# A linear-attention, gated-MLP and mixer kernel: state products on quarter tiles behind a TensorE drain, and preparation work moved between VectorE, ScalarE and GpSimd

## The chip, the core and the metric

One NeuronCore of one Trainium2 chip. The metric is the device time of one execution in microseconds (us), the median of several runs. All times here are in us unless ns is written. The engines are TensorE (PE, with its weight loads as PEld), VectorE (DVE), ScalarE (ACT), GpSimd (POOL) and SyncE (SP), whose queue issues the DMAs.

## What is computed

Three modules in a chain. The first is a linear attention with a forget gate, for 4 batches of 8 heads, 768 tokens and 48 columns a head:

```python
f = 1.0 / (1.0 + np.exp(-f_logit))
for t in range(S):
    state = f[:, :, t, :, None] * state + np.einsum('bhd,bhe->bhde', k[:, :, t], v[:, :, t])
    y[:, :, t] = np.einsum('bhd,bhde->bhe', q[:, :, t], state)
```

The second is a gated MLP over tokens: `h = relu(x @ w_in)` is split into `u` and `v`, `v` is normalised over its 512 columns, mixed over the tokens as `w_spatial @ v_n + b_spatial`, multiplied by `u`, and multiplied by `w_out`. The third is a mixer: `u = x + (relu(x^T @ w_tok1) @ w_tok2)^T`, then `u + relu(u @ w_ch1) @ w_ch2`, with 384 model columns, 256 token columns and 1536 channel columns.

## The kernel before

**Precision.** A product of two f32 matrices is made of three fast matmuls: each operand is split into a high part (rounded to the fast type) and a low part (what the rounding left), and L196, L197 and L198 issue high by high, low by high and high by low. Some small products in the attention run in plain f32, each as two matmul records in the trace.

**Weights.** They arrive as 64-bit numbers. `rounded` turns a piece of 128 x 384 of them into f32: a DMA of 384 KB, two VectorE instructions (L74, L77), one on ScalarE (L81), one on GpSimd (L83). Then ScalarE writes the high part (L156) and the engine that `split_weight` is given writes the low part (L159). The staging buffers `wst` and `wsa` are rings of three. Some weights are rounded early and stored back to DRAM as f32 by `round_weight` (w_tok1, w_tok2 and w_ch1; the tasks are called `later`), and loaded again, at half the bytes, where they are split (kind "narrow").

**Attention.** The work is cut into 32 units of one batch, one half of the sequence (six chunks of 64 tokens) and one pair of heads (`unit(k)`). Per unit, VectorE scans the gates (L332, L346) and scales `kq` (L352); TensorE makes `products`, `turns` and `keys`; ScalarE copies the products out (`am`, L393), GpSimd masks them (L398). VectorE sums the states chunk by chunk (L412). GpSimd multiplies all of a unit's states by the gates at the chunk ends and lays them out as block-diagonal matrices of both heads in `now` (L420, with a second multiplicand `pown` written by L340). On TensorE `past` (L429) multiplies `now` by the queries, one 112 x 112 matmul a chunk, five chunks in the first half of a sequence and six in the second. `sums` (L440) adds the part within the chunk to the same PSUM tile `py`. ScalarE and VectorE split the result into high and low (L461, L465).

The small products use the array as four quarter tiles of 64 x 64: `block(old, now, new)` issues `past` of one unit first, then walks round robin over four lists with the products and turns of a later unit, the keys of the next, and the sums. A chain on one quarter tile thus runs beside those on the other three.

**Order.** `settle` is a planner: every piece of work is a task with an engine, a cost, a rank and the buffers that it takes; the planner plays the queues forward and emits the task of lowest rank among those that can start soonest. Attention, gated MLP and weight pieces are mixed by it. `s1_tasks` makes the first half of the gated MLP: relu on ScalarE (`r`, L710), its statistics on VectorE (L714, L716), the inverse root on GpSimd (L722), the normalised `vf` on VectorE (L726), then high part `vh` on ScalarE (L734) and low part `vl` on VectorE (L737). The mix follows: `g` (L807, L808), `gh` (L813), `gl` (L818). The last stage (c1, c2, ff) is emitted in the order of the code, with weight pieces woven in by `staged`.

Every engine runs its instructions in the order in which they were emitted.

Of the kernel before, what the change touches and what calls it, by code (L numbers as in the profile page):

```python
# [9 lines left out]
F32 = mybir.dt.float32  # L10
# [9 lines left out]
def tile_kernel(ctx, tc, fkqs, v, w_in, w_sp, b_sp, w_out, w_t1, w_t2, w_c1, w_c2, out):  # L20
# [179 lines left out]
    def body(general):  # L200
# [42 lines left out]
        now = attp.tile([P, NT, 2, 64], F32, name="now")  # L243
        zs = [attp.tile([P, NT, D], F32, name=f"zs{i}") for i in range(NP)]
        own = attp.tile([P, 1, 2], F32, name="own")
        pown = attp.tile([P, B * NP, 2 * NT, 2], F32, name="pown")
        for t in [first, last, now, own]:
            nc.gpsimd.memset(t, 0.0)
        for j in range(2):
            nc.gpsimd.memset(own[64 * j : 64 * j + 64, :, j], 1.0)  # L250
# [13 lines left out]
        def scanned(u, b, hf, p, fs, kq, vt):  # L264
# [9 lines left out]
            vs = at2.tile([P, W], F32, tag="am", name=f"vs{u}")  # L274
# [31 lines left out]
        def unit(k):  # L306
# [30 lines left out]
            def ends():  # L337
                end = d["pg"][:, 1, T - 1 :: T]
                nc.gpsimd.tensor_copy(pend[:, b * NP + p, n0 : n0 + NT], end)
                nc.gpsimd.tensor_tensor(  # L340
                    out=pown[:, b * NP + p, n0 : n0 + NT], in0=end.unsqueeze(2).to_broadcast([P, NT, 2]),
                    in1=own.to_broadcast([P, NT, 2]), op=ALU.mult,
                )
# [73 lines left out]
            def scaled(eng):  # L417
                n = NT - 1 + hf
                x = n0 - hf
                eng.tensor_tensor(  # L420
                    out=now[:112, 1 - hf :, :, :D], in0=d["z"][:112, :n].unsqueeze(2).to_broadcast([112, n, 2, D]),
                    in1=pown[:112, b * NP + p, x : x + n].unsqueeze(3).to_broadcast([112, n, 2, D]), op=ALU.mult,
                )

            def past():

                py = d["py"]
                for c in range(1 - hf, NT):
                    nc.tensor.matmul(  # L429
                        py[:112, c % 2, c // 2 * T : (c // 2 + 1) * T],  # L430
                        now[:112, c].rearrange("p j e -> p (j e)")[:, :112], d["qi"][:112, toks(c)],
                        start=c + hf < 3, stop=False, skip_group_check=True,
                    )

# [53 lines left out]
        def block(old, now, new):  # L488
# [3 lines left out]
            if old:  # L492
                old["d"]["py"] = ps_y.tile([P, 2, 512], F32, tag="py", name="py")
                old["past"]()
# [6 lines left out]

            if new:
# [3 lines left out]
            if now:  # L506
                now["d"]["pk"] = pa
                add(now["keys"])
            if old:
                add(old["sums"])  # L510
            run(*tiles[::2], *tiles[1::2])
# [61 lines left out]
        def att_tasks(k, at):  # L573
# [18 lines left out]
            else:  # L592
                task(f"G{k}", "ACT", 0.65, at - 3.2, f["gate"], [f"L{k}", back1("SC")])
                task(f"SC{k}", "DVE", 1.17, at - 3, f["ahead"], [f"G{k}", back1("BK")], [("pg", 1, [f"MU{k}", f"PE{k}"])])
                task(f"PE{k}", "POOL", 0.45, at - 2.8, f["ends"], [f"SC{k}"])
# [3 lines left out]
                for r in range(2):  # L599
# [6 lines left out]
                eng, ns = "POOL", 1.4  # L606
                task(
                    f"NW{k}", eng, ns, at + 3, partial(f["scaled"], nc.gpsimd), [f"ST{k}"],
                    [("now", 1, [f"SU{k}"])],
                )  # L610
# [51 lines left out]
        def piece_tasks(name, gen, rank, width, kind, ring=True, after=()):  # L662
# [4 lines left out]
            if kind == "narrow":  # L667
                task(f"{name}d", "SP", 0.45, rank, step, after, kb=192 * r, rings=[("wsa", 3, [f"{name}l"])])
                task(f"{name}h", "ACT", 0.45 * r, rank + 2, step, [f"{name}d"])
                task(f"{name}l", "POOL", 1.05 * r, rank + 2, step, [f"{name}h"])  # L670
# [3 lines left out]
            last_use = {"pe": f"{name}t", "pool": f"{name}l", "store": f"{name}s"}[kind]  # L674
# [10 lines left out]
            else:  # L685
                task(f"{name}l", "POOL", 1.05 * r, rank + 1, step, [f"{name}h"])
# [4 lines left out]
        def s1_tasks(b, hf, places):  # L691
# [6 lines left out]
            def norm(i):  # L698
# [19 lines left out]
                def root():  # L718
# [3 lines left out]
                    nc.gpsimd.tensor_tensor(out=e["rs"], in0=ve, in1=nhalf, op=ALU.pow)  # L722

                def full():
                    e["vf"] = rp.tile([P, DH], F32, tag="vf", name=f"vf{b}{hf}{i}")
                    nc.vector.tensor_scalar(  # L726
                        out=e["vf"], in0=e["r"], scalar1=e["mv"][:, 0:1], scalar2=e["rs"], op0=ALU.subtract, op1=ALU.mult
                    )
# [20 lines left out]
                task(f"RS{n}", "POOL", 0.85, t - 3, root, [f"BN{n}"])  # L749
                task(f"VF{n}", "DVE", 0.55, t - 1, full, [f"RS{n}"], [("vf", 2, [f"VL{n}"])])  # L750
# [442 lines left out]
```

## Time and profile before

| what | value |
|---|---|
| median of 3 runs | 784.16 us (782.85 to 785.61) |
| the profiled execution | 782.59 us |
| its span, first to last instruction | 780.9 us |
| TensorE busy | 731.0 us, 94% |
| VectorE, ScalarE, GpSimd busy | 432.6, 248.8, 440.3 us |
| TensorE's mean granted clock | 0.975 |

Busy times are sums of instructions over the whole span and hide that the stages differ. The program has a lead-in of some 116 us, in which attention units start without much other work to fill TensorE; a packed stretch up to about 360 us with attention, gated MLP and weight pieces together; a change-over to the last stage up to 456 us; and a last stretch that is almost only TensorE. The profiled execution's own time is 1.6 us under the median.

### The profile page before, as it was taken

How to read it: one execution, taken by the hardware profiler on the slowest of the kernel's cores; microseconds unless marked ns; L12 is line 12 of the kernel's file. 1: busy time of each engine (PE TensorE's matmuls, PEld its weight loads, DVE VectorE, ACT ScalarE, POOL GpSimd, SP SyncE). 2: the span in 40 equal slices, each digit the busy share in tenths (PEclk: the TensorE clock that was granted, in tenths of full speed). 3: DMA queues.
4: the chain of work that ended last, by engine and by line, in shares of the span. 5: the costliest groups of instructions: out<-in, count | busy, mean ns of one | idle time of the engine just before them, and what ended most of it. 6: DMA issues, size and time to landing. Idle time of an engine off the chain costs nothing.

```text
span 780.9 us, 16957 instructions
## 1 busy us (share of the span) xinstructions
PE 731.0 (94%) x6853; PEld 707.9 (91%) x6853; DVE 432.6 (55%) x799; ACT 248.8 (32%) x532; POOL 440.3 (56%) x610
## 2 busy tenths in 40 slices
PE   2787889998999989999999899999999999999996
PEld 2677789997999879999989899999999999999996
DVE  7998799999998967663554842231212212231222
ACT  4554342443433442234534521231112211111111
POOL 5687673566645643233834896649456693548420
PEclk9897899999999999999999999999999999999999
DMA  7445532757455641202532623142211422113111
GB/s 274 117 146 165 187 89 88 209 144 217 153 163 171 200 128 47 62 14 78 161 111 64 227 59 118 42 131 72 85 58 31 142 82 92 41 37 107 58 34 37
DMA packets 53065, 86.65 MB, mean 111 GB/s; under 512 B 6000, under 2 KB 41584, under 8 KB 52976
## 3 DMA queue, kind: packets, MB, share of 16 engines
q1 hardware_dynamic: 52976, 85.47, 36.0%
q8 instruction: 56, 0.92, 0.5%
q14 instruction: 33, 0.27, 0.1%
HBM read 69.71 MB, written 13.37 MB: 106 GB/s over the span
## 4 chain that ended last, share of the span: by engine, by line
PE 67%; DVE 7%; DMA 5%; POOL 3%; issue 2%; ACT 2%; SPq 0%; DVEq 0%; POOLq 0%; ACTq 0%
PE po L1072 18%; PE p L198 8%; PE p L197 8%; PE p L196 8%; PE ps L196 3%; PE ps L198 3%; PE ps L197 3%; PE py L429 2%; PE px L196 2%; PE px L198 2%; PE px L197 2%; PE pa L361 1%; PE pu L196 1%; PE py L440 1%; PE pu L197 1%
## 5 line engine op out<-in xcount | busy, mean ns | idle before, releaser
L1060 DVE SCALAR_TENSOR_TENSOR hl<-p,hh 128x384 fp32r<-128x384 f32 x96 | 53.4, 557 | 174.2 <-ACT hh L1059 164.1
L1059 ACT ACTIVATE hh<-p 128x384 fp32r<-128x384 f32 x96 | 47.1, 492 | 185.6 <-PE p L198 185.5
L1072 PE MATMUL po<-hl,wc2h 128*128 128x384 f32 x288 | 96.5, 335 | 3.7 <-DVE hl L1060 3.7
L1072 PE MATMUL po<-hh,wc2l 128*128 128x384 f32 x288 | 96.3, 334 | 0.0
L1072 PE MATMUL po<-hh,wc2h 128*128 128x384 f32 x288 | 75.0, 336 | 0.0
L136 POOL TENSOR_SCALAR look<-look 128x192 f32<-128x192 f32 x88 | 63.5, 722 | 7.6
L135 POOL TENSOR_TENSOR look<-look 128x192 f32<-128x192 f32 x88 | 45.9, 524 | 38.6 <-DMA look<-in_w_c 25.1
L398 POOL TENSOR_SCALAR_AFFINE_SELECT am<-am 64x384 f32<-64x384 f32 x64 | 41.6, 650 | 42.7 <-ACT am L393 38.9
L196 PE MATMUL ps<-wsph,vh 128*128 128x384 f32 x192 | 65.4, 341 | 0.0
L198 PE MATMUL p<-uh,wc1l 128*128 128x384 f32 x192 | 64.5, 336 | 0.0
L197 PE MATMUL p<-ul,wc1h 128*128 128x384 f32 x192 | 64.5, 336 | 0.0
L198 PE MATMUL ps<-wsph,vl 128*128 128x384 f32 x192 | 64.4, 335 | 0.0
L197 PE MATMUL ps<-wspl,vh 128*128 128x384 f32 x192 | 64.3, 335 | 0.0
L196 PE MATMUL p<-uh,wc1h 128*128 128x384 f32 x192 | 64.0, 336 | 0.0
L1083 POOL TENSOR_TENSOR us<-uh,ul 128x384 f32<-128x384 f32 x24 | 25.0, 1049 | 61.7 <-DVE ul L1043 52.4
L1072 PEld LDWEIGHTS po<-hl,wc2h 128*128 128x128 f32 x288 | 54.1, 188 | 4.4 <-DVE hl L1060 4.4
L137 POOL TENSOR_TENSOR lows<-lows,look 128x192 f32<-128x192 f32 x88 | 53.3, 606 | 6.2
L1072 PEld LDWEIGHTS po<-hh,wc2l 128*128 128x128 f32 x288 | 54.0, 188 | 0.0
L1072 PEld LDWEIGHTS po<-hh,wc2h 128*128 128x128 f32 x288 | 52.6, 189 | 0.0
L429 PEld LDWEIGHTS py<-kq,now 112*112 112x112 f32 x352 | 41.5, 189 | 9.0 <-POOL now L420 8.5
L429 PE MATMUL py<-kq,now 112*112 112x64 f32 x352 | 42.4, 273 | 6.5 <-POOL now L420 6.5
L361 PE MATMUL pa<-kq 48*64 48x64 f32 x768 | 20.3, 241 | 25.7 <-DVE kq L352 7.8
(391 smaller groups left out, 1977.7 us busy)
## 6 DMA issues: line engine op xcount, KB each, us to landing
kq<-in_fkq SPq DMA_DIRECT2D x32, 384.0 KB, 4.3
look<-in_w_c SPq DMA_DIRECT2D x48, 192.0 KB, 2.4
fs<-in_fkq SPq DMA_DIRECT2D x32, 195.5 KB, 3.7
vt<-in_v SPq DMA_DIRECT2D x8, 576.0 KB, 6.4
x1d<-xs SPq DMA_DIRECT2D x24, 192.0 KB, 2.1
xf<-x1d SPq DMA_DIRECT2D x12, 384.0 KB, 4.4
out<-ot SPq DMA_DIRECT2D x24, 192.0 KB, 2.0
look<-in_w_in SPq DMA_DIRECT2D x16, 192.0 KB, 3.0
```

The source lines that it names most:

```text
L135: nc.gpsimd.tensor_tensor(out=hi, in0=hi, in1=hi, op=ALU.mult)
L136: nc.gpsimd.tensor_scalar(out=hi, in0=hi, scalar1=NEAR**2, scalar2=None, op0=ALU.is_lt)
L137: nc.gpsimd.tensor_tensor(out=to, in0=to, in1=hi, op=ALU.add)
L196: nc.tensor.matmul(ps, lh, rh, start=first and i == 0, stop=False, **kw)
L197: nc.tensor.matmul(ps, lh, rl, start=False, stop=False, **kw)
L198: nc.tensor.matmul(ps, ll, rh, start=False, stop=i == n - 1, **kw)
L361: nc.tensor.matmul(d["pa"][span(r, T), j, i * T : (i + 1) * T], d["ki"][span(j), toks(c)], d["qi"][span(j), toks(c)], start=True, stop=True,)
L398: nc.gpsimd.affine_select(out=am, in_=am, compare_op=ALU.is_ge, fill=0.0, base=T * r, pattern=[[0, 2], [0, NCW], [1, T]], channel_multipli ...
L429: nc.tensor.matmul(py[:112, c % 2, c // 2 * T : (c // 2 + 1) * T], now[:112, c].rearrange("p j e -> p (j e)")[:, :112], d["qi"][:112, toks ...
L1059: nc.scalar.activation(hh, ps, AF.Relu)
L1060: nc.vector.scalar_tensor_tensor(out=hl, in0=ps, scalar=0.0, in1=f32(hh), op0=ALU.max, op1=ALU.subtract)
L1072: nc.tensor.matmul(po[c], l[:, ft, csl], r, start=ft == 0 and x == 0, stop=ft == NF - 1 and x == 2)
```

## The change

1. **State products.** `now` holds one 64-wide matrix per chunk and no zeros of a second head. `past(j)` is a generator that multiplies each head's 48 rows on a quarter tile of its own (row tile j, column tile j). Both generators are put at the head of the lists of quarter tiles 0 and 2, so that they run round robin with the products, turns and keys. Behind all of these stands `nc.tensor.drain()`, and the sums follow as a round of their own.
2. **Scaled states** (`scaled`, task NW) go from GpSimd to VectorE, with half the elements; `own`, `pown` and the instruction that wrote it go.
3. **Normalisation** (`full`, task VF) goes from VectorE to ScalarE, as an activation with scale and bias; GpSimd gets one more small instruction (`nb`) for the bias.
4. **w_ch1** is no longer rounded early and stored; its twelve pieces are rounded where they are split: six as tasks (kind "pool") of the last planned stage, six in `staged`. Each then loads 384 KB where it loaded 192.
5. **Low parts** of w_spatial (12 pieces) and w_out (4 pieces) go from GpSimd to VectorE (kind "own"); the pieces of w_out are ranked four places earlier.
6. A buffer tag of a path that these inputs don't take.

The core of the diff:

```diff
-            def scaled(eng):
+            def scaled():
                 n = NT - 1 + hf
                 x = n0 - hf
-                eng.tensor_tensor(
-                    out=now[:112, 1 - hf :, :, :D], in0=d["z"][:112, :n].unsqueeze(2).to_broadcast([112, n, 2, D]),
-                    in1=pown[:112, b * NP + p, x : x + n].unsqueeze(3).to_broadcast([112, n, 2, D]), op=ALU.mult,
-                )
-
-            def past():
-
-                py = d["py"]
+                nc.vector.tensor_tensor(
+                    out=now[:112, 1 - hf :, :D], in0=d["z"][:112, :n],
+                    in1=pend[:112, b * NP + p, x : x + n].unsqueeze(2).to_broadcast([112, n, D]), op=ALU.mult,
+                )
+
+            def past(j):
+
+                m = D if j else T
                 for c in range(1 - hf, NT):
                     nc.tensor.matmul(
-                        py[:112, c % 2, c // 2 * T : (c // 2 + 1) * T],
-                        now[:112, c].rearrange("p j e -> p (j e)")[:, :112], d["qi"][:112, toks(c)],
-                        start=c + hf < 3, stop=False, skip_group_check=True,
-                    )
+                        d["py"][64 * j : 64 * j + m, c % 2, c // 2 * T : (c // 2 + 1) * T], now[span(j), c, :m],
+                        d["qi"][span(j), toks(c)], start=c + hf < 3, stop=False, skip_group_check=True,
+                    )
+                    yield
...
-                old["past"]()
             tiles = [[], [], [], []]
...
+            if old:
+                for j in range(2):
+                    tiles[2 * j].append(old["past"](j))
...
+            run(*tiles[::2], *tiles[1::2])
             if old:
+                nc.tensor.drain()
+                tiles = [[], [], [], []]
                 add(old["sums"])
-            run(*tiles[::2], *tiles[1::2])
+                run(*tiles)
...
-                eng, ns = "POOL", 1.4
-                task(
-                    f"NW{k}", eng, ns, at + 3, partial(f["scaled"], nc.gpsimd), [f"ST{k}"],
-                    [("now", 1, [f"SU{k}"])],
-                )
+                task(f"NW{k}", "DVE", 0.38, at + 3, f["scaled"], [f"ST{k}"], [("now", 1, [f"SU{k}"])])
...
-                    nc.vector.tensor_scalar(
-                        out=e["vf"], in0=e["r"], scalar1=e["mv"][:, 0:1], scalar2=e["rs"], op0=ALU.subtract, op1=ALU.mult
-                    )
+                    nc.scalar.activation(e["vf"], e["r"], AF.Identity, bias=e["nb"], scale=e["rs"])
...
-        for name, src in (("wt1", w_t1), ("wt2", w_t2), ("wc1", w_c1)):
+        for name, src in (("wt1", w_t1), ("wt2", w_t2)):
...
-            piece_tasks(f"wc{n}", x, place + 1.5 * n, WST, "narrow")
+            piece_tasks(f"wc{n}", x, place + 1.5 * n, WST, "pool")
```

What the change moves, at three places. First TensorE, the start of a block in the packed stretch (`kq` the queries and keys, `pa` the PSUM of products, turns and keys, `am` the masked products, `vt` the values). Before:

```order
L429 MATMUL py<-kq_1179,now 112x64 x5
L361 MATMUL pa<-kq_1457 64x64 x12
L371 MATMUL pa<-ident,kq_1457 64x48 x8
L371 MATMUL pa<-ident,kq_1457 64x64 x4
L384 MATMUL pa<-vt_928,am_1634 64x48
```

and after:

```order
L421 MATMUL py<-kq_1041,now 64x64
L421 MATMUL py<-kq_1041,now 48x64
L353 MATMUL pa<-kq_1240 64x64 x2
L421 MATMUL py<-kq_1041,now 64x64
L421 MATMUL py<-kq_1041,now 48x64
L353 MATMUL pa<-kq_1240 64x64 x2
L421 MATMUL py<-kq_1041,now 64x64
L421 MATMUL py<-kq_1041,now 48x64
L353 MATMUL pa<-kq_1240 64x64 x2
L421 MATMUL py<-kq_1041,now 64x64
L421 MATMUL py<-kq_1041,now 48x64
L363 MATMUL pa<-ident,kq_1240 64x48 x2
```

The state products were five matmuls in a row ahead of the block; they are ten quarter-tile matmuls between the products (L353) and turns (L363) of tiles 1 and 3. The drain prints no row; it stands behind the last of the keys, ahead of the first of the sums.

Second, ScalarE at the place that ran from 274 to 283 us (`wc10d` pieces of w_ch1 on their way to DRAM, `wc2` pieces of w_ch2, `am`, `y`, `fs` and `first` attention, `r` the relu of the gated MLP). Before:

```order
L81 ACTIVATE wc10d21152st<-wc10d21152st 128x384
L461 CAST y_3948<-py 112x384
L393 COPY am_3955<-pa 128x704
L81 ACTIVATE wc220st<-wc220st 128x384
L710 ACTIVATE r_3980<-pv_3937 128x512
L710 ACTIVATE r_4001<-pv_3962 128x512
```

and the same relu after:

```order
L385 COPY am_4005<-pa 128x704
L453 CAST y_4020<-py 112x384
L707 ACTIVATE r_4044<-pv_4009 128x512
L707 ACTIVATE r_4069<-pv_4033 128x512
L321 ACTIVATE fs_4002<-fs_4002 128x385
L323 ACTIVATE first<-fs_4002 128x6
```

The pieces of w_ch1 and w_ch2 (L81) that stood ahead of `r` are gone from this place; the first of them now stands in the last mix.

Third, VectorE in the last mix of the gated MLP. Before:

```order
L807 TENSOR_TENSOR g_5290<-ps_5237,bb 128x384
L808 TENSOR_TENSOR g_5290<-g_5290,u_4852 128x384
L818 TENSOR_TENSOR gl_5295<-g_5290,gh_5294 128x384
L807 TENSOR_TENSOR g_5319<-ps_5270,bb 128x384
L808 TENSOR_TENSOR g_5319<-g_5319,u_5075 128x384
L74 TENSOR_SCALAR wc200sa<-wc200st 128x384
L807 TENSOR_TENSOR g_5336<-ps_5300,bb 128x384
L77 SCALAR_TENSOR_TENSOR wc200sa<-wc200st,wc200sa 128x384
L74 TENSOR_SCALAR wc210sa<-wc210st 128x384
L808 TENSOR_TENSOR g_5336<-g_5336,u_5075 128x384
L77 SCALAR_TENSOR_TENSOR wc210sa<-wc210st,wc210sa 128x384
L74 TENSOR_SCALAR wc220sa<-wc220st 128x384
```

and after:

```order
L807 TENSOR_TENSOR g_5380<-g_5380,u_4959 128x384
L74 TENSOR_SCALAR wc1x00sa<-wc1x00st 128x384
L77 SCALAR_TENSOR_TENSOR wc1x00sa<-wc1x00st,wc1x00sa 128x384
L817 TENSOR_TENSOR gl_5392<-g_5380,gh_5391 128x384
L806 TENSOR_TENSOR g_5416<-ps_5360,bb 128x384
L807 TENSOR_TENSOR g_5416<-g_5416,u_4959 128x384
L817 TENSOR_TENSOR gl_5424<-g_5416,gh_5423 128x384
L74 TENSOR_SCALAR wc10384sa<-wc10384st 128x384
L77 SCALAR_TENSOR_TENSOR wc10384sa<-wc10384st,wc10384sa 128x384
L806 TENSOR_TENSOR g_5450<-ps_5397,bb 128x384
L807 TENSOR_TENSOR g_5450<-g_5450,u_5197 128x384
L74 TENSOR_SCALAR wc11384sa<-wc11384st 128x384
```

Before, the pieces of w_ch2 came here, three in all. Now nine pieces of w_ch1 stand ahead of them, each as a pair of L74 and L77 between `g` and `gl`, and the three of w_ch2 follow.

## Rows read from the trace of the kernel before

PE, PEld, DVE, ACT, POOL are TensorE's matmuls and weight loads, VectorE, ScalarE and GpSimd. In a timeline the columns are start and duration in us, engine, line, operation, output and inputs, and count; in brackets stands how long the engine was idle ahead of it and what it waited for.

**Rows 1.** The page: busy us, share of the span and instructions by engine.

```profile
PE 731.0 (94%) x6853; PEld 707.9 (91%) x6853; DVE 432.6 (55%) x799; ACT 248.8 (32%) x532; POOL 440.3 (56%) x610
```

**Rows 2.** Per stretch: length, busy us of PE, PEld, DVE, ACT, POOL; clock; DMA share; GB/s.

```profile
0.00:116.00 116.00, 84.57 (x1274) 75.48 (x1274) 97.66 (x172) 55.07 (x127) 79.77 (x113) 0.90 0.53 165
...
360.00:456.00 96.00, 90.96 (x509) 88.50 (x508) 60.74 (x86) 42.68 (x88) 63.33 (x63) 0.98 0.42 129
```

**Rows 3.** What TensorE waited for: total us, times, longest.

```profile
PE py L429 <- POOL now L420: 6.5, 5, 2.9
...
PE pu L196 <- ACT r L710: 2.4, 1, 2.4
```

**Rows 4.** TensorE's timeline, a block with five chunks of state products: start, duration (us).

```profile
125.72 1.10 PE L429 MATMUL py<-kq,now 112*112 112x64 f32 x10
126.76 0.58 PE L361 MATMUL pa<-kq 48*64 48x64 f32 x24
127.16 0.53 PE L371 MATMUL pa<-ident,kq 48*64 48x48 f32 x24
127.51 0.46 PE L384 MATMUL pa<-vt,am 64*64 64x48 f32 x22
127.78 0.22 PE L440 MATMUL py<-am,vt 64*48 64x64 f32 x1
...
127.84 0.55 PE L440 MATMUL py<-am,vt 64*48 64x64 f32 x22
128.32 0.44 PE L196 MATMUL ps<-wsph,vh 128*128 128x384 f32 x1
128.60 0.33 PE L197 MATMUL ps<-wspl,vh 128*128 128x384 f32 x1
```

**Rows 5.** The same view, the state products of a block with six chunks.

```profile
175.71 1.30 PE L429 MATMUL py<-kq,now 112*112 112x64 f32 x12
```

**Rows 6.** ScalarE's timeline, the reader of the products' result in the block at 125 us.

```profile
128.45 0.48 ACT L461 CAST x<-py 112x384 fp32r<-112x384 f32 x1 [0.83 <-PE py L440]
```

**Rows 7.** Groups: line, operation, count, busy us, mean ns, idle before (the last: 0 to 113 us).

```profile
L420 POOL TENSOR_TENSOR now<-zs,pown 112x576 f32<-112x576 f32 x16 | 26.5, 1656 | 8.7 <-DVE zs L412 8.7
...
L159 POOL TENSOR_TENSOR wspl<-wspsa,wsph 128x384 fp32r<-128x384 f32 x12 | 14.0, 1172 | 1.5 <-ACT wsph L156 1.5
...
L412 DVE SCALAR_TENSOR_TENSOR zs<-zs,pend,pa 112x48 f32<-112x48 f32 x80 | 21.1, 264 | 2.9
...
L726 DVE TENSOR_SCALAR vf<-r,mv,rs 128x512 f32<-128x512 f32 x6 | 6.1, 1009 | 2.6 <-POOL rs L722 2.6
```

**Rows 8.** VectorE's timeline at 62 us, one operation twice.

```profile
62.04 0.54 DVE L726 TENSOR_SCALAR vf<-r,mv,rs 128x512 f32<-128x512 f32 x1
63.04 1.21 DVE L726 TENSOR_SCALAR vf<-r,mv,rs 128x512 f32<-128x512 f32 x1 [0.47 <-POOL rs L722]
```

**Rows 9.** Around 180 and 280 us: VectorE, TensorE and ScalarE timelines; then two stretches as above.

```profile
182.11 0.27 DVE L412 SCALAR_TENSOR_TENSOR zs<-z,pend,pa 112x48 f32<-112x48 f32 x1
...
183.21 1.00 PE L429 MATMUL py<-kq,now 112*112 112x64 f32 x8 [2.87 <-POOL now L420]
...
281.91 0.55 ACT L81 ACTIVATE wc220st<-wc220st 128x384 uint32<-128x384 uint32 x1 [5.92 <-DMA wc220st<-in_w_c]
...
180.00:200.00 20.00, 17.13 (x262) 15.26 (x262) 18.05 (x39) 8.56 (x20) 13.57 (x18) 0.91 0.75 222
200.00:220.00 20.00, 20.00 (x208) 19.86 (x207) 18.98 (x40) 7.00 (x17) 12.59 (x13) 1.00 0.44 130
```

**Rows 10.** VectorE in the last mix: its sum over 28 us, then three of its instructions.

```profile
380.00:408.00 28.00, 17.99 (x27) 1.00 0.40 113
...
395.86 0.35 DVE L74 TENSOR_SCALAR wc210sa<-wc210st 128x384 uint32<-128x384 uint32 x1
...
398.30 1.27 DVE L77 SCALAR_TENSOR_TENSOR wc220sa<-wc220st,wc220sa 128x384 uint32<-128x384 uint32 x1
399.49 0.55 DVE L818 TENSOR_TENSOR gl<-g,gh 128x384 fp32r<-128x384 f32 x1
```


## What the change will do to the time

> **What bounds the kernel now.** I read the page's busy shares first: TensorE is busy 731.0 of 780.9 us, VectorE and GpSimd little over half [rows 1]. So a us taken out of TensorE's own work in a full stretch is a us gained, and work moved between the other engines counts only where TensorE waits for them. Next came the sums by stretch [rows 2]. In the first 116 us TensorE is busy 84.57, at a granted clock of 0.90, and VectorE 97.66: the lead-in belongs to VectorE, with GpSimd at 79.77 beside it. From 360 to 456 us TensorE lacks 5 us. The list of TensorE's waits [rows 3] says for whom: 6.5 us in five waits for GpSimd's `now`, 2.4 for the relu `r`. Last I read TensorE's timeline inside one block of the packed stretch [rows 4] and the places of the longest waits [rows 9].
>
> **State products on quarter tiles.** Of the 32 blocks I counted 23 in the packed stretch, 12 with five chunks and 11 with six. In one with five, the products start at 125.72 and the next form at 126.76: 1.04 us for ten records; twelve take about 0.2 more, 1.30 against 1.10 [rows 4, 5]. Quarter-tile records are cheaper: 24 of them, six rounds of four tiles, take 0.35 us (127.16 to 127.51), 58 ns a round [rows 4]. After the change ten more records stand on tile 0 and ten on tile 2, beside those of 1 and 3, so the block grows by ten rounds (twelve with six chunks): 0.58 (0.70) us. The switch of tile size, which was between L429 and L361, moves to the block's start; I charge 0.10 for it, since going back costs 0.28 against the 0.17 of a normal step [rows 4]. So 1.04 - 0.58 - 0.10 = 0.36, and 1.24 - 0.70 - 0.10 = 0.44 gross.
>
> Against it stands the drain. No row shows one in the middle of work. What it must wait for is the last key's end: a quarter-tile matmul lasts 0.22 us [rows 4], and the reader of the sums on ScalarE starts at 128.45 [rows 6], 0.06 after their shown end of 127.84 + 0.55 [rows 4]. From the last start that is 0.28; 0.06 of it would have passed anyway, and some 0.05 to fill the array again comes on top: 0.27. If the sequencer only held until the last columns had streamed it would be two rounds, about 0.12; if the flush also stopped the loading of weights, half as much again, 0.41. I take 0.27, the middle, nearest to the row that ends in a reader. Net per block -0.09 and -0.17, over 23 blocks -1.1 - 1.9 = **-3.0 us**, with ends of -6.5 (0.12) and +0.3 (0.41). The nine blocks of the lead-in are hidden by VectorE.
>
> One thing about the tiles isn't in any row: in the blocks now, records that run at once on different row tiles write different PSUM banks, while both heads' state products go to bank c % 2 together. The Trainium skill ("TensorEngine Tiling (Array Packing)", Gotcha 1 under Restrictions and Gotchas) says that different row tiles cannot access the same PSUM bank simultaneously; no run here shows it yet, and by that rule the gain would turn into the loss of the second rival below.
>
> **Scaled states, normalisation, low parts.** `now` took 1.66 us on GpSimd [rows 7]. On VectorE it has 288 elements a partition, between one state step of 48 (0.26 us, rows 7) and a 384-wide pass (0.55, rows 10); I take 0.4. In order it stands directly behind its states, so the hand-over to a busy GpSimd goes. At 180 us the states end at 182.38 and TensorE starts at 183.21 [rows 9]: with 0.4 behind the states it would start at about 182.7, -0.5. TensorE still waits over 2 us there, so I leave that gap's clock alone. The four shorter waits for `now` (3.6 us together, rows 3) lie mostly in the lead-in; I count 0.6.
>
> The wait for `r` at 280 us is another thing. ScalarE stood 5.92 us at a piece of w_ch2 whose DMA had not come, with `r` queued behind it [rows 9]. In the new order no weight piece stands on ScalarE there, since w_ch1's stores are gone and w_ch2's first pieces come later. That returns 2.4 us and what the clock lost behind it: after the equal gap at 180 the stretch has 0.91 of 20 us, the next 1.00 [rows 9], so 1.8 lost, of which I take 1.5. Packed stretch: -0.5 - 0.6 - 2.4 - 1.5 = **-5.0 us**; ends 0 (each gap is filled by the next late thing) and -9 (all waits for `now` go, and the 1.8 at 180).
>
> **The lead-in.** VectorE gets, ahead of the first gated addition: 16 low parts of 0.55 (12 of w_spatial, 4 of w_out) = 8.8; ten `now` of 0.4 = 4.0; it loses six `vf`, 6.1 [rows 7]. One `kq` pass of about 1 us also comes earlier. Net +7.7. Against that GpSimd loses ten times 1.66 and 16 times 1.17 [rows 7], 35 of some 80 us. The two engines hinder each other: the same `vf` takes 0.54 and 1.21 us [rows 8], and six of them 6.1 where 3.3 would do. With VectorE busy 84% of the lead-in, about 30 of those 35 us ran beside VectorE's work; if that work gained a quarter of it, 7.5 us come back. The 2.6 us that VectorE waited for `rs` ahead of `vf` [rows 7] also go, and ScalarE, busy 55 of 116 us, has room for `vf`. I take **0**, with ends of -6 and +8.
>
> **The last mix.** Between 380 and 408 us VectorE is busy 17.99 of 28 [rows 10]. Nine pieces of w_ch1 come into it. One piece costs VectorE 0.35 + 0.55 alone and up to 0.35 + 1.27 beside GpSimd [rows 10]: 8.1 to 14.6 us, into 10.0 free ones. The pieces stand in order between `g` and `gl`, and each L74 waits for a 384 KB load in a ring of three, so `gl`, for which TensorE's next product waits, queues behind them; on ScalarE `gh` queues behind L81 in the same manner. Three more pieces come behind it, in the first products of the last stage. I take **+3.5 us**: 2 of overrun and 1.5 of lowered clock; ends 0 and +10. What these pieces cost before (twelve passes through VectorE, ScalarE, GpSimd and two DMAs in the packed stretch) was hidden by TensorE's work, so its removal counts only through the gap at 280.
>
> **Sum.** -3.0 - 5.0 + 0 + 3.5 = -4.5 against the profiled execution's 782.6, so 778.1. That execution is 1.6 under the median of 784.16; the median after comes to **about 779.6 us**.
>
> **Rivals.** All are against the median.
> - *The drain takes back what the tiles give* (0.41 and more): block term 0 in place of -3.0, so 782.6. For it: no overlap can cross a drain, and the gross gain is only 0.4 a block. Against: the row of the reader bounds it at 0.28. 0.14.
> - *Two row tiles on one bank take turns.* Then the state products of the two heads don't overlap: 10 or 12 rounds of 58 ns more, 0.58 or 0.70 us, over 23 blocks +14.7, so 794: slower. This is the mechanism of the rule named above. It decides from about a third of that on. For it: both halves of a chunk are issued back to back to one bank. Against: they write different partitions of it. 0.07.
> - *VectorE in the lead-in doesn't get its relief*: the low parts and `now` cost 7.7 and nothing comes back, so TensorE's full stretch begins 8 us later: 787.5, slower. For it: VectorE is busy 97.66 of the 116 us [rows 2], so little of 7.7 finds a pause. It decides where the relief is under 2 us. Against: the two prices of `vf` [rows 8]. 0.14.
> - *The last mix overruns by 10*: 786, same or slower. For it: three more engines get longer there at once. 0.10.
> - *The waits go altogether* (-9) and the drain is short: 772. 0.13.
>
> **Numbers.** My forecast holds 0.42. A measurement of this kernel can tell 0.3% from no change, 2.4 us: faster is under 781.8, slower over 786.5. Faster: 0.36 of the forecast, the last rival's 0.13 and 0.04 of the first, 0.53. Same: 0.05 + 0.09 + 0.02 of the lead-in's + 0.06 of the last mix's, 0.22. Slower: the rest, 0.25. The range reaches from the good rival's 770 to just past the lead-in's, 789.
>
> **What would show it.** Right: in a block, L421 and L353 share a stretch of about 1.7 us, then a hole of some 0.27 before L432; no wait for `now` over 2.3; the relu at 280 without its gap; the packed stretch beginning within 3 us of 116; VectorE nearly full from 380 to 408, with small waits of TensorE for `gl` or `gh`. Wrong: rounds of state products over 100 ns (the bank), a hole of 0.4 or more (the drain), VectorE's lead-in longer by 8, or new waits of TensorE in the last stage of more than 6 us together.

## The result and the profile after

The changed kernel takes 774.34 us (773.29 to 775.48) where the kernel before took 783.5 in the same measurement: a ratio of 0.988 with a 95% interval of 0.9854 to 0.9906, or -9.2 us. The profiled execution of after took 775.48 us with a span of 773.7, 7.2 under the span of before. The traces differ by that much.

The page and the sums by stretch of after, to be set beside [rows 1, 2] (busy us of PE, PEld, DVE, ACT, POOL, then clock, DMA share, GB/s):

```profile
PE 724.3 (94%) x7205; PEld 691.1 (89%) x7205; DVE 421.3 (54%) x823; ACT 265.2 (34%) x556; POOL 369.4 (48%) x551
```

```profile
0.00:116.00 116.00, 88.62 (x1513) 78.12 (x1514) 99.11 (x211) 61.33 (x139) 47.42 (x81) 0.91 0.54 171
...
360.00:456.00 96.00, 88.00 (x485) 84.06 (x484) 72.36 (x98) 41.50 (x87) 72.36 (x67) 0.96 0.47 146
```

GpSimd has lost 71 us, 32 of them in the first 116 us; VectorE has gained next to nothing there (99.11 against 97.66), in spite of what was moved to it. TensorE is busy 88.62 there in place of 84.57: its packed stretch began earlier. From 360 to 456 it is the other way round, 88.00 and a clock of 0.96.

The waits of TensorE in after, beside [rows 3]:

```profile
PE px L196 <- DVE g L806: 6.6, 3, 4.3
PE py L421 <- DVE now L412: 3.8, 3, 2.4
```

and the one of before for `g`:

```profile
PE px L196 <- DVE g L807: 0.9, 1, 0.9
```

`now` still stops TensorE for 3.8 us (before 6.5), `r` not at all (before 2.4), and `g` of the last mix does so for 6.6 (before 0.9).

Where the 7.2 us lie can be read from the starts of the same blocks in both TensorE timelines, numbered 1 to 32 in order. The table gives the start before and the shift of after in us; a falling row is time gained since the row above.

| TensorE's work | before | after |
|---|---|---|
| block 11 (lead-in's end, 5 chunks) | 125.7 | -9.4 |
| block 23 (6 chunks) | 254.9 | -9.7 |
| block 25 (5 chunks) | 271.5 | -11.1 |
| block 26, behind the former wait for `r` | 287.8 | -15.2 |
| last state products | 351.8 | -15.8 |
| last mix begins | 371.2 | -16.0 |
| last product of the gated MLP | 416.7 | -6.7 |
| end | 780.9 | -7.2 |

So the lead-in gave 9.4 us, the packed stretch 6.4, and the last mix took 9.2 back.

### The profile page after: what moved, and what is told of

It is laid out like the page before. It is cut to its first block, busy times and chain, and to the rows that moved or that the text cites. A ratio compares the mean times of both kernels' runs of the same rounds, so it can differ in the third digit from the quotient of the medians.

```text
span 773.7 us, 17638 instructions
## 1 busy us (share of the span) xinstructions
PE 724.3 (94%) x7205; PEld 691.1 (89%) x7205; DVE 421.3 (54%) x823; ACT 265.2 (34%) x556; POOL 369.4 (48%) x551
## 4 chain that ended last, share of the span: by engine, by line
PE 73%; DVE 10%; DMA 5%; POOL 4%; issue 4%; ACT 3%; SPq 0%; DVEq 0%; POOLq 0%; ACTq 0%
PE po L1071 17%; PE p L198 7%; PE p L197 7%; PE p L196 7%; PE ps L196 3%; PE ps L198 3%; PE ps L197 3%; PE pv L196 2%; PE px L196 2%; PE py L432 2%; PE py L421 2%; PE pv L197 2%; PE pv L198 2%; PE px L198 2%; PE px L197 2%
## 5 line engine op out<-in xcount | busy, mean ns | idle before, releaser
L390 POOL TENSOR_SCALAR_AFFINE_SELECT am<-am 64x384 f32<-64x384 f32 x64 | 39.8, 621 | 67.3 <-ACT am L385 65.0
L353 PE MATMUL pa<-kq 48*64 48x64 f32 x768 | 32.6, 243 | 21.5 <-issue 8.5
L335 POOL COPY pend<-pg 128x6 f32<-128x6 f32 x32 | 9.5, 297 | 81.9 <-DVE pg L328 81.0
L353 PEld LDWEIGHTS pa<-kq 48*64 48x64 f32 x768 | 26.4, 152 | 23.1 <-issue 8.9
```

The lines of the kernel that those rows point to most:

```text
L353: nc.tensor.matmul(d["pa"][span(r, T), j, i * T : (i + 1) * T], d["ki"][span(j), toks(c)], d["qi"][span(j), toks(c)], start=True, stop=True,)
L390: nc.gpsimd.affine_select(out=am, in_=am, compare_op=ALU.is_ge, fill=0.0, base=T * r, pattern=[[0, 2], [0, NCW], [1, T]], channel_multipli ...
```

## The experiments

Times are medians. The ratio is to the kernel before on the same chip, with its 95% interval. The last two columns are the shifts of blocks 11 and 18 against before.

| run | what | us | ratio to before | block 11 | block 18 |
|---|---|---|---|---|---|
| after | the changed kernel | 774.3 | 0.9880 (0.9854 to 0.9906) | -9.4 | -9.2 |
| two_drains | a second drain | 774.6 | 0.9888 (0.9833 to 0.9942) | -10.4 | -10.0 |
| b_tiles | before, with quarter tiles and drain | 777.4 | 0.9944 (0.9920 to 0.9969) | -2.5 | -3.5 |
| noise | large extra GpSimd work in the lead-in | 784.7 | 1.0022 (0.9997 to 1.0047) | +0.1 | +0.7 |
| pow | small-data extra GpSimd work | 783.3 | 1.0012 (0.9983 to 1.0041) | +1.0 | +1.2 |
| r_scaled | `now` back on GpSimd | 774.8 | 0.9914 (0.9875 to 0.9953) | -8.9 | -9.1 |
| r_low | low parts back on GpSimd | 775.2 | 0.9892 (0.9831 to 0.9953) | -9.4 | -7.1 |
| r_both | both back | 777.6 | 0.9945 (0.9919 to 0.9970) | -5.0 | -5.1 |
| r_vf | `vf` back on VectorE | 773.0 | 0.9893 (0.9849 to 0.9937) | -9.2 | -8.2 |
| r_wc1 | w_ch1 rounded early again | 772.0 | 0.9849 (0.9801 to 0.9897) | -11.5 | -11.6 |
| wc1_vf | the last two together | 771.3 | 0.9859 (0.9796 to 0.9921) | -9.5 | -8.9 |
| early | six pieces ahead of the last mix | 774.8 | 0.9921 (0.9892 to 0.9950) | -8.2 | -8.0 |
| hybrid | nine pieces early, three late | 767.1 | 0.9815 (0.9752 to 0.9877) | -10.3 | -10.2 |

The runs were measured in groups on different chips: the kernel before took 780.8 us beside b_tiles, r_scaled, r_vf and early, 782.9 beside the others, and 783.5 beside after. Where times of different groups are set against each other, the ratio decides. Kernels whose order in the lead-in is that of the changed one (two_drains, early, after) differ by 2 us in their shifts, so a single us decides nothing.

**The drain: two_drains.**

```diff
                 nc.tensor.drain()
+                nc.tensor.drain()
```

> The changed kernel with two drains in a row. If the 0.30 us hole behind the last of the keys is the emptying of the array, the second drain finds it empty and costs under 0.05 us a block: time 774 to 775.5. If it is a fixed price of the instruction, the hole doubles, 0.28 us more in each of 24 blocks: time 780 to 782.

A block of after (start, duration in us; L421 the state products, L353 and L363 products and turns, L376 the keys, L432 the sums):

```profile
124.95 0.34 PE L198 MATMUL ps<-wsph,vl 128*128 128x384 f32 x1
125.22 0.27 PE L421 MATMUL py<-kq,now 48*64 48x64 f32 x2
125.23 0.27 PE L353 MATMUL pa<-kq 48*64 48x64 f32 x2
125.32 0.23 PE L421 MATMUL py<-kq,now 48*48 48x64 f32 x2
125.34 0.23 PE L353 MATMUL pa<-kq 48*64 48x64 f32 x2
125.37 0.23 PE L421 MATMUL py<-kq,now 48*48 48x64 f32 x2
...
126.52 0.53 PE L376 MATMUL pa<-vt,am 64*48 64x48 f32 x10
127.13 0.58 PE L432 MATMUL py<-am,vt 64*64 64x64 f32 x24
127.64 0.44 PE L196 MATMUL px<-wouth,gh 128*128 128x384 f32 x1
```

and the same place with two drains:

```profile
125.61 0.52 PE L376 MATMUL pa<-vt,am 64*48 64x48 f32 x10
126.30 0.58 PE L432 MATMUL py<-am,vt 64*64 64x64 f32 x24 [0.16 <-issue]
126.80 0.44 PE L196 MATMUL px<-wouth,gh 128*128 128x384 f32 x1
```

The state products step by 0.05 to 0.06 us, two row tiles at once on one bank. The hole: the last of the ten keys from 126.52 on starts at 126.83, and the sums begin at 127.13, 0.30 later (0.30 to 0.33 in 21 of the 22 blocks from 116 us on); before, the sums began 0.00 to 0.04 after a key in most blocks. The second drain adds 0.08 to each hole, more than the 0.05 that I had allowed and far from the doubling of a fixed price. I read it as 0.08 for a drain that finds nothing to wait for, and the rest of the 0.3 as the waiting for the array. The median moved by 0.3 us, less than its spread. From the start of the last 128-row matmul to the start of the first one behind the block, before took 2.77 us with five chunks and 2.94 with six, after 2.70 and 2.80: 0.07 and 0.14 gained, 2.4 us over the ten and twelve blocks from block 11 on.

**The tiles alone: b_tiles.** The functions `past`, `scaled` and `block` of the change in the kernel before, `now` on GpSimd:

```diff
-                eng, ns = "POOL", 1.4
...
+                task(f"NW{k}", "POOL", 0.75, at + 3, f["scaled"], [f"ST{k}"], [("now", 1, [f"SU{k}"])])
```

> The kernel before with the first part of the change alone: state products on quarter tiles, drain, sums as their own round; `now` stays on GpSimd, with half its elements. If the block's gain is what the trace of the changed kernel shows, 0.07 us with five chunks and 0.14 with six, it is 2.4 us in the packed stretch; `now` at half size takes 0.5 to 0.7 us less on GpSimd each time, which is worth 1 to 4 us in the lead-in. Time 777 to 781. If the drain ate the gain, 782 to 784.

The ratio to before is 0.9944 (0.992 to 0.9969), 4.4 us; the trace is 3.7 shorter. Its blocks take 2.70 and 2.80 us, as in after, so the block's gain is the tiles' own. Block 11 comes 2.5 us earlier, in the lead-in, where I had counted the tiles and the smaller `now` at nothing; that is little more than the 2 us by which equal lead-ins differ. By the last state products only 1.4 of it were left: at 270 us TensorE waited 5.24 us for `now`, after ScalarE had stood 5.12 at a piece of w_ch2. So how the 4.4 us are made up isn't settled.

**What shortened the lead-in: noise, pow, r_scaled, r_low, r_both.** The extra work of noise stands behind each of the first ten `now` and each of the sixteen low parts:

```diff
+                if k < 10 and not general:
+                    nc.gpsimd.tensor_tensor(out=spare[:112, :576], in0=spare[:112, :576], in1=spare[:112, :576], op=ALU.mult)
```

> The changed kernel with 26 extra GpSimd instructions in the lead-in that nobody reads: ten of 112x576 (the size that GpSimd's `now` had) and sixteen of 128x384 (the size of a low part), some 30 us; every other engine keeps its order. Theory A, that the lead-in became 9 us shorter because VectorE is less hindered by GpSimd: the scans, `kq` and `vl` on VectorE get dear again, the first gated addition comes at 109 to 113 us in place of 104.5, and the time is 779 to 783 us. Theory B, that the gain is one of order (`now` directly behind its states, `vf` off VectorE, w_out's pieces earlier): the first gated addition stays at 104 to 106, and the time at 774 to 776.

and in pow:

```diff
+                    for i in range(3):
+                        nc.gpsimd.tensor_tensor(out=spare[:, i : i + 1], in0=spare[:, 9:10], in1=nhalf, op=ALU.pow)
```

> The run with extra GpSimd work in the lead-in again, but each extra 112x576 or 128x384 instruction (about 1.5 and 1.0 us) is replaced by three or two instructions on 128x1 (0.57 us each in the kernel before): the same 33 us on GpSimd, with hardly any data. Theory A1, VectorE is hindered by GpSimd's data traffic: with none, the lead-in is that of the changed kernel, time 774 to 777. Theory A2, what counts is GpSimd's queue (masks and chunk ends behind other work): the lead-in is as long as with the large instructions, time 782 to 785.

Both cancel the lead-in's gain, but not in the same way. In noise the first gated addition came at 116.9 us (104.5 in after, 112.8 before) and the time above theory A's 783; yet the scans stayed cheap (1009 and 979 ns), which theory A had dear. VectorE's groups up to 105 us (count, busy us, mean ns) in after, noise and pow, in this order:

```profile
L328 DVE TENSOR_TENSOR_SCAN pg<-fs,first 128x384 f32<-128x384 f32 x12 | 12.1, 1007 | 5.8 <-ACT first L323 4.4 <-DVE kq L344 0.8 <-issue 0.6
...
L338 DVE TENSOR_TENSOR_SCAN pg<-fs,last 128x384 f32<-128x384 f32 x12 | 11.5, 961 | 0.1
L159 DVE TENSOR_TENSOR wspl<-wspsa,wsph 128x384 fp32r<-128x384 f32 x12 | 6.5, 568 | 0.6 <-ACT wsph L156 0.6
...
L412 DVE TENSOR_TENSOR now<-z,pend 112x240 f32<-112x240 f32 x6 | 2.8, 461 | 0.0
```

```profile
L159 DVE TENSOR_TENSOR wspl<-wspsa,wsph 128x384 fp32r<-128x384 f32 x12 | 9.1, 784 | 0.6 <-ACT wsph L156 0.6
L416 DVE TENSOR_TENSOR now<-z,pend 112x240 f32<-112x240 f32 x5 | 5.8, 1169 | 0.0
```

```profile
L159 DVE TENSOR_TENSOR wspl<-wspsa,wsph 128x384 fp32r<-128x384 f32 x12 | 6.3, 550 | 0.6 <-ACT wsph L156 0.6
...
L417 DVE TENSOR_TENSOR now<-z,pend 112x240 f32<-112x240 f32 x5 | 3.4, 671 | 0.0
```

Large data beside it stretches VectorE's low part from 568 to 784 ns and `now` from 461 to 1169; powers of 128x1 leave the low part at 550, and the 671 of `now` comes from one of 1.75 us beside four of 0.40 to 0.41. The powers act through GpSimd's own queue. Its chunk ends (`pend`), up to 105 us in after and up to 117 in pow, then two of the extra groups:

```profile
L335 POOL COPY pend<-pg 128x6 f32<-128x6 f32 x12 | 3.7, 307 | 22.7 <-DVE pg L328 22.7
```

```profile
L162 POOL TENSOR_TENSOR spare<-spare,nhalf 128x1 f32<-128x1 f32 x32 | 24.0, 771 | 0.0
L423 POOL TENSOR_TENSOR spare<-spare,nhalf 128x1 f32<-128x1 f32 x30 | 23.4, 802 | 0.0
...
L340 POOL COPY pend<-pg 128x6 f32<-128x6 f32 x12 | 5.3, 440 | 8.0 <-DVE pg L333 8.0
```

In after GpSimd stood idle 22.7 us ahead of the chunk ends, ready for them; in pow 8.0. From the end of a gate scan to the end of its chunk ends, summed over twelve units, it took 8.0 us in after, 19.5 before, 23.3 in pow, and 10.1 in noise. Two reservations. The small instructions took 0.79 us on average and not 0.57, so pow puts 47 us on GpSimd and not 33: it was busy 84.2 of the first 105 us, where before it was 70.3 and after 46.2. So pow shows that the queue can cost the whole gain, not that the queue of before did. And late chunk ends are not enough: in r_low they sum to 15.6 us, in r_vf to 13.4, and block 11 comes as early as in after.

Undoing one part at a time:

```diff
-                nc.vector.tensor_tensor(
+                nc.gpsimd.tensor_tensor(
```

> The changed kernel with `now` back on GpSimd, at half its former elements. Theory of the hand-over: each block of the lead-in waits for GpSimd again, some 0.5 to 1 us for each of ten, first gated addition at 108 to 112, time 778 to 783. Theory of hindrance: ten instructions of about 0.8 us on GpSimd in place of 0.46 on VectorE cost next to nothing, first gated addition at 103.5 to 106, time 773 to 776.

```diff
-            piece_tasks(f"wsp{n}", x, -18 + n * 1.2, WST, "own", after=[f"SU{NP - 1}"])
+            piece_tasks(f"wsp{n}", x, -18 + n * 1.2, WST, "narrow", after=[f"SU{NP - 1}"])
...
-            piece_tasks(f"wout{n}", x, -2 + n, WST, "own")
+            piece_tasks(f"wout{n}", x, 2 + n, WST, "pool")
```

> The changed kernel with the 16 low parts of w_spatial and w_out back on GpSimd and w_out at its old rank. Theory A (hindrance): VectorE loses 9.4 us of work in the lead-in and gets some 19 us of GpSimd work beside it, so the two nearly cancel: first gated addition at 103 to 107, time 773 to 777. Theory B (order): w_out comes late again, the wait for its high part (3.5 us) is back, first gated addition or first product behind it 3 to 5 us later, time 777 to 780.

and both:

> The changed kernel with both the 16 low parts and `now` (half size) back on GpSimd; each alone moved the time by under 1 us. If what counts is the sum of GpSimd's work in the lead-in, the two together cost more than the two apart: the blocks from 125 us on come 5 to 8 us later than in the changed kernel and the time is 779 to 782. If the parts are independent, 1 to 3 us later in the packed stretch, and 774 to 776.5.

Both times, 774.8 and 775.2, fall in the ranges of hindrance. Against after, `now` alone costs 0.34%, 2.7 us, the low parts alone 0.12%, 0.9 us, and both together (777.6) 0.65%, 5.1 us; the intervals are 0.3 to 0.6% to either side, so the times alone don't show that the parts fail to add up. By the medians themselves the three are 0.5, 0.9 and 3.2 us. Block 11 comes 4.4 us later with both back, block 18 4.1 later (0.1 for `now`, 2.1 for the low parts). r_low moves more than block 11 tells: its first gated addition comes at 110.3 us, later than both theories had it. r_low and r_both also put w_out back to its old rank, so engine and order are not told apart there. In r_both the scans are dear again:

```profile
L328 DVE TENSOR_TENSOR_SCAN pg<-fs,first 128x384 f32<-128x384 f32 x12 | 14.5, 1206 | 7.0 <-ACT first L323 5.1 <-POOL am L390 1.0 <-DVE kq L344 0.8
L338 DVE TENSOR_TENSOR_SCAN pg<-fs,last 128x384 f32<-128x384 f32 x11 | 13.7, 1245 | 0.3
```

against 1007 and 961 ns in after (1220 and 1276 before, in the same view up to 113 us). With one part back they stay cheap: 1005 and 963 ns in r_low, 970 and 1014 in r_scaled. So on VectorE's scans the two parts act together. The time, 777.6, lies between the two forecasts, and the blocks came a little less late than the 5 to 8 us of the first.

**`vf`: r_vf.**

```diff
-                    nc.scalar.activation(e["vf"], e["r"], AF.Identity, bias=e["nb"], scale=e["rs"])
+                    nc.vector.tensor_scalar(
+                        out=e["vf"], in0=e["r"], scalar1=e["mv"][:, 0:1], scalar2=e["rs"], op0=ALU.subtract, op1=ALU.mult
+                    )
```

> The changed kernel with the normalised `vf` back on VectorE and the bias instruction gone from GpSimd. Six of them stand in the lead-in. If VectorE's sum of work sets the lead-in, 3.3 us (at 0.54) come on top and the wait for the inverse root is back on VectorE (1 to 2.5 us): first gated addition at 107 to 110, time 777 to 780. If not, 104 to 105.5 and 774 to 775.5.

773.0 us (772.0 to 774.4), under both forecasts, a ratio of 0.9893 where after has 0.9880: this part of the change brings nothing that can be measured.

**w_ch1: r_wc1, wc1_vf, early, hybrid.**

```diff
-        for name, src in (("wt1", w_t1), ("wt2", w_t2)):
+        for name, src in (("wt1", w_t1), ("wt2", w_t2), ("wc1", w_c1)):
...
-            piece_tasks(f"wc{n}", x, place + 1.5 * n, WST, "pool")
+            piece_tasks(f"wc{n}", x, place + 1.5 * n, WST, "narrow")
```

> The changed kernel with w_ch1 rounded early and stored again, as before. If the nine pieces in the last mix are what gave 9 us back there, the 4.3 us wait for `g` goes and the last mix is 8 to 10 us shorter. The packed stretch takes the pieces again: if they are hidden there but for ScalarE's wait at a late load, 3 to 5 us come back at about 270 to 290, and the time is 768 to 771. If their removal was the cause of more (VectorE and GpSimd relieved in the packed stretch), it is 775 to 778.

770.9 to 772.8 in its runs, where the changed kernel had 773.3 to 775.5; between the two forecasts. The last mix, from its start to the last product of the gated MLP, took 45.4 us before, 54.6 in after and 46.4 here. In after, TensorE's longest wait there and VectorE ahead of it:

```profile
396.40 0.69 PE L196 MATMUL px<-wouth,gh 128*128 128x384 f32 x1 [4.30 <-DVE g L806]
...
389.05 1.85 DVE L817 TENSOR_TENSOR gl<-g,gh 128x384 fp32r<-128x384 f32 x2
391.81 1.15 DVE L74 TENSOR_SCALAR wc1x0768sa<-wc1x0768st 128x384 uint32<-128x384 uint32 x1 [0.91 <-POOL wc1xl L159]
392.99 1.24 DVE L77 SCALAR_TENSOR_TENSOR wc1x0768sa<-wc1x0768st,wc1x0768sa 128x384 uint32<-128x384 uint32 x1
394.15 0.35 DVE L74 TENSOR_SCALAR wc200sa<-wc200st 128x384 uint32<-128x384 uint32 x1
394.53 1.35 DVE L77 SCALAR_TENSOR_TENSOR wc200sa<-wc200st,wc200sa 128x384 uint32<-128x384 uint32 x1
395.80 0.55 DVE L806 TENSOR_TENSOR g<-ps,bb 128x384 f32<-128x384 f32 x1
```

TensorE's last product before that wait ended at 392.1. VectorE stood at pieces of w_ch1 and w_ch2: it waited 0.91 us for a staging buffer that GpSimd's low part still held, and then worked 4 us on two pieces. Only then came `g` (L806), which reads the PSUM tile of the mix; in the code `ps` and `px` share a ring of three PSUM tiles, so the next `px` could not start before. The stretches of the last mix (before, after, r_wc1, hybrid):

```profile
371.00:417.00 46.00, 44.67 (x257) 44.00 (x256) 23.29 (x33) 17.88 (x36) 23.36 (x20) 1.00 0.41 124
```

```profile
355.00:410.00 55.00, 48.01 (x255) 45.77 (x254) 40.13 (x51) 24.16 (x51) 34.44 (x30) 0.94 0.52 158
```

```profile
361.00:408.00 47.00, 44.87 (x257) 44.19 (x256) 22.55 (x33) 18.50 (x38) 24.27 (x21) 1.00 0.40 122
```

```profile
354.00:403.00 49.00, 45.16 (x255) 43.84 (x254) 28.14 (x39) 21.07 (x44) 28.23 (x24) 1.00 0.48 154
```

40.13 against 22.55: 17.6 us of VectorE work came into it, and the clock fell to 0.94. The nine pieces of w_ch1 are 16.6 us of it: six of their L77 took 1.24 to 1.38 us and three 0.56, and five of their L74 took 1.14 to 1.18, four 0.35. The dear L74 was there before:

```profile
393.50 1.15 DVE L74 TENSOR_SCALAR wc200sa<-wc200st 128x384 uint32<-128x384 uint32 x1 [2.17 <-POOL wc1l L159]
```

But r_wc1 pays elsewhere. ScalarE in its packed stretch:

```profile
257.79 0.55 ACT L81 ACTIVATE wc200st<-wc200st 128x384 uint32<-128x384 uint32 x1 [5.00 <-DMA wc200st<-in_w_c]
...
269.79 0.56 ACT L81 ACTIVATE wc220st<-wc220st 128x384 uint32<-128x384 uint32 x1 [7.83 <-DMA wc220st<-in_w_c]
```

It stood 5.0 and 7.8 us at w_ch2's first pieces, which, with the staging ring free, are emitted there; before, that was the 5.92 us of [rows 9]. The packed stretch lost 6 us by it: the last mix begins 10.0 us earlier than before, not 16.0, though block 11 came 11.5 earlier. With `vf` back as well:

> The changed kernel with two of its parts undone: w_ch1 rounded early as before, and `vf` on VectorE. Alone they gave 772.0 and 773.0 us. If their gains add, 770 to 771.5; if the packed stretch, where both put work on VectorE, takes it back, 772 to 775.

771.3, inside the first forecast; but its runs (770.4 to 772.6) are those of r_wc1 over again, and the ratios, 0.9859 and 0.9849, show no gain from `vf`. The next run moved six pieces ahead of the last mix, into the planned part that fills 340 to 360 us:

```diff
+        for n, x in enumerate([x for i in range(3) for x in st_c[i::4]]):
+            piece_tasks(f"we{n}", x, place + 2 + n, WST, "pool")
```

> The changed kernel with six of w_ch1's pieces moved out of the last mix into the planned part just ahead of it, where VectorE is busy 6 of 20 us (340 to 360 us); three pieces stay in the last mix. If VectorE's queue between `g` and `gl` is what stops TensorE there, the waits for `g` (6.6 us) fall under 2 and the clock behind them stays up: 7 to 9 us less, time 765 to 768. If the load of 384 KB or the ring of three is the limit, the pieces only stop the engines earlier: time 772 to 776.

774.8, the second forecast. VectorE and TensorE there:

```profile
367.34 1.98 DVE L74 TENSOR_SCALAR wc10384sa<-wc10384st 128x384 uint32<-128x384 uint32 x1 [7.86 <-POOL wc1l L159]
...
374.72 0.55 PE L1033 MATMUL p<-ident,xf 128*128 128x128 f32 x3 [2.52 <-DVE h1l L1010]
...
382.42 0.44 PE L196 MATMUL ps<-wsph,vh 128*128 128x384 f32 x1 [2.47 <-DVE g L806]
```

VectorE was free for 7.86 us and waited for a staging buffer held by a low part on GpSimd; TensorE waited for the mixer's first stage instead, and the last mix took 57.4 us. That low part stood behind two instructions of the mixer on GpSimd (`x1l`, 3.67 us together). The limit is the ring of three and the queue behind it, not VectorE's time. Last, only the three pieces of the first column block late:

```diff
         return dst, [
             partial(piece, i, c0, min(WST, cols - c0)) for i in range(rows // P) for c0 in range(0, cols, WST)
+            if name[:3] != "wc1" or c0
...
+            if raw is not None and c0 == 0:
+                rawr = raw.bitcast(U32).rearrange("(n p) c -> n p c", p=P)
+                a = yield from rounded(stage, rawr[first + i], c0, width, f"{name}{i}{c0}", tiny, st)
...
-            piece_tasks(f"wc{n}", x, place + 1.5 * n, WST, "pool")
+            piece_tasks(f"wc{n}", x, place + 1.5 * n, WST, "pool" if n < NK else "narrow")
```

> The changed kernel with nine of w_ch1's twelve pieces rounded early and stored as before, and only the three of the first column block rounded in the last mix. With all twelve early, ScalarE stood 5.0 and 7.8 us at w_ch2's first pieces in the packed stretch, which were emitted there because the staging ring was free; the three late pieces hold that ring until the last mix. If that wait is what the early rounding costs, the packed stretch is as short as in the changed kernel (last mix from about 354 to 357 us) and the last mix as short as before (46 to 49 us): time 766 to 769. If the stores themselves cost the packed stretch its time, 771 to 774.

767.1 us (766.2 to 768.4), a ratio of 0.9815 to before (0.9752 to 0.9877): 5 us less than the changed kernel by the ratios, 7 by the medians, with the last mix from 354.0 us on and 48.7 long. No piece of w_ch2 stands on ScalarE from 255 to 285 us now, and its longest wait there is another:

```profile
281.40 0.52 ACT L816 CAST gh<-g 128x384 fp32r<-128x384 f32 x1 [3.13 <-DVE g L811]
```

So the early rounding and the stores of nine pieces are hidden; what early rounding cost in r_wc1 was ScalarE's place in the queue. Three pieces fewer are rounded early than in r_wc1; what that alone is worth no run tells.

## Why the prediction came out as it did

The sign, the range and the block's mechanism held. Two terms were mis-sized in opposite directions.

- **State products.** Forecast -3.0; the blocks gave 2.4, as 0.07 and 0.14 where 0.09 and 0.17 stood. From block 11 on there are 22, ten with five chunks and twelve with six; I had counted 23. The drain's hole was 0.28 net where 0.27 was forecast; of its terms, the 0.05 for filling the array again is shown by no run, only the hole as a whole. The bank rival fell: the rule of the Trainium skill ("TensorEngine Tiling (Array Packing)", Gotcha 1) does not show here for two row tiles that write different partitions of one bank: the rounds took 0.05 to 0.06 us, as rounds on different banks do, and the measurement decides.
- **Packed stretch.** Forecast -5.0; -6.4 together with the blocks' 2.4, so -4.0. That is the wait for `r`: it went, and returned 4.1 between blocks 25 and 26, where 3.9 was forecast. The 1.1 forecast for `now` doesn't show. Its longest wait fell from 2.9 to 2.4, the forecast 0.5, but behind it the clock was 0.66 from 170 to 180 us (before, 0.83 from 180 to 190), and from block 11 to block 23 the shift grew by 0.3 where the blocks alone give 1.3; 1.1 came back by block 25, where two shorter waits for `now` had been.
- **Lead-in.** Forecast 0, with an end of -6; measured -9.4. This step failed. VectorE's added work was sized well (`now` 0.46 where 0.4 stood, the low parts 0.57 where 0.55 did). What was missing: I set the tiles of the lead-in's blocks and the smaller `now` at nothing (2.5 us at block 11, b_tiles), and I saw GpSimd's lost work only as a relief for VectorE, worth the work that VectorE got. With the low parts and `now` back on GpSimd, 4.4 us of the 9.4 are gone (r_both, w_out's rank included). The rest, some 2.5, stays open. So does the way in which GpSimd's work acts. In its own queue the chunk ends of the lead-in come 11.5 us earlier in sum and the masks 4.6 (24.5 us from the end of ScalarE's copy to the mask's before, 19.9 after, over eleven units), and pow shows that a queue fuller than that of before can undo the gain; but r_low has late chunk ends and an early block 11, and r_both has VectorE's dear scans as well.
- **The last mix.** Forecast +3.5, end +10; measured +9.2. The step that failed is the price of the pieces on VectorE: L74 was taken at 0.35 throughout, but took 1.14 to 1.18 in five of nine, so they cost 16.6 us and not 8.1 to 14.6, against 10.0 free ones; and each of three staging buffers was held until GpSimd's low part. TensorE stood idle 5.7 us more than before and worked 3.3 longer at the lower clock, where 2 and 1.5 were forecast. The pieces in VectorE's order were the cause that I named, but TensorE waited for `g`, and through it for a PSUM tile, not for `gl` or `gh`.

The two errors left the sum 4.7 us too high against the medians (-4.5 forecast, -9.2 measured). Part of that, 2.0 us, is that the profiled executions differ by only 7.2. That the sum came so near is in part luck: the lead-in gave 9.4 more than forecast and the last mix took 5.7 more, and the two stand against each other. Of the signs named for being right, three did not come: a wait for `now` was 2.4 and not under 2.3, the packed stretch began 9 us earlier and not within 3, and the waits in the last mix, 6.6 us, were not small.

## What to carry to other kernels

Where one engine serves a chain in small steps (masks, chunk ends) and also does bulk work, taking the bulk work off it can count although it is not the bottleneck: here 4.4 us at a GpSimd that was busy 70 of 105 us. Its price is read by putting the work back, not from the busy time, and not from how late the small steps come either. Work on a staging ring is emitted by this planner as soon as a buffer is free, not when it is needed, and an instruction that waits there for its load blocks everything behind it in its queue: a ring kept busy a little longer can be worth more than the work saved. Several moves off one engine need not add up: undo them together before calling one of them useless.

## What the runs showed of the hardware

A drain of TensorE between quarter-tile rounds leaves a hole of 0.30 to 0.33 us from the last start to the next; a second one adds 0.08. Two row tiles that write different partitions of one PSUM bank keep the step of 0.05 to 0.06 us. GpSimd's 128x1 powers mostly took 0.57 us or a little less, in the kernel before and in pow, with a mean of 0.71 before and 0.79 in pow; they left VectorE's 128x384 subtraction at 0.55, while GpSimd's 128x384 subtraction took the same VectorE instruction to 0.78.
